# Windowed attention and a gated feed-forward layer on one core: new start-up order for loads, casts, exponentials and masks

## The chip, the core and the metric

The kernel runs on one core of a Trainium2 chip. The metric is the time of one execution on the device in microseconds. The kernel before took 253.31 us, the median of 3 runs (253.07 to 253.32). The profiled execution spans 251.2 us from its first to its last recorded instruction; the times of rows below are counted from the start of that span.

Five engines work at the same time, each through its own queue in order: TensorE (PE; its weight loads are PEld), VectorE (DVE), ScalarE (ACT), GpSimd (POOL) and SyncE (SP). Instructions wait for each other through semaphores.

## The reference, cut to what matters

Two layers follow each other. The first is attention with 4 batches, 8 heads, 768 positions and 64 values a head. A query sees the first 8 positions and the last 96 up to itself; a bias grows with the distance, with its own slope in each head. The second is a feed-forward layer over 3072 tokens with 512 features and 1536 hidden ones.

```python
scores = scale * np.matmul(q, k.transpose(0, 1, 3, 2))
...
keep = is_global | is_local
dist = np.where(is_global & ~is_local, float(n_local), np.abs(rel))
slopes = 2.0 ** (-8.0 * (np.arange(H) + 1) / H)
scores = np.where(keep, scores - slopes[:, None, None] * dist, -1e9)
a = softmax(scores)                        # cut: max, exp, sum written out in the reference
x = np.matmul(a, v)                        # heads side by side: 3072 x 512
gate = np.maximum(x @ w_gate, 0.0)
out = (gate * (x @ w_val)) @ w_out
```

## The kernel before

The sequence of a batch is cut into two halves of 384 queries, so there are eight half-sequences, numbered s = 0 to 7. Heads are taken in pairs p = 0 to 3. Attention of one half is woven into the feed-forward matmuls of an earlier half. At the start there is nothing to weave it into, and the code below lays out by hand in which order every engine works. "Pair" below is a pair of heads of half 0 if nothing else is said.

Loads of half 0, a k and a q transfer for each pair, all from SyncE's queue:

```python
        for src, dst in ((k, ks_of[s]), (q, qs_of[s])):
            nc.sync.dma_start(
                out=dst[:, h0:h1, :],
                in_=src[b, h0:h1, half * QH : (half + 1) * QH, :].rearrange(
                    "h (p n) d -> p h (n d)", n=NN))
```

The pieces for a pair: cast k and q to bf16 (L255), transpose them on TensorE into a PSUM bank (L290), copy the transposed keys (L270 to L272) and queries (L300) to SBUF on VectorE, start the scores' PSUM banks with the distance bias (a matmul of a scaled identity with the distances, L312), add the score matmuls onto them (L330), and take the exponential (L335):

```python
    def piece_cast(s, p, i, eng):
        if (s, p) not in cast_of:
            cast_of[s, p] = cast_pool.tile([128, 2, NN, 2, D], BF16, name="qk")
        src = (qs_of[s], ks_of[s])[i]
        (eng.copy if eng is nc.scalar else eng.tensor_copy)(
            cast_of[s, p][:, i].rearrange("t n e d -> t e n d"),
            src[:, 2 * p : 2 * p + 2, :].rearrange("t e (n d) -> t e n d", n=NN))
...
    def piece_copy(s, p):
        b, half = divmod(s, 2)
        tp = tp_of[s, p]
        put_keys(nc.vector.tensor_copy, nc.vector.tensor_copy, kT[b % 2][p], tp[:, 1, :], half)
        for e in range(2):
            r = slice(64 * e, 64 * e + 64)
            nc.vector.tensor_copy(qTb[s % 2][r, p, e, :], tp[r, 0, :])
...
    def piece_bias(s, p):
        pool, name = (ff_psum, "ff_ps") if s == 0 and p % 2 else (qk_psum, "qk_ps")
        banks = [pool.tile([128, 512], FP32, name=name) for _ in range(3)]
        qk_of[s, p] = banks
        for g, bank in enumerate(banks_of_half[s % 2]):
            c = 0
            for i, (j, a, w, m) in enumerate(bank):
                for e in range(2):
                    nc.tensor.matmul(banks[g][:, c : c + NN * w], lhsT=sid[:, 2 * p + e],
                                     rhs=dd[:, 0 if j == 0 else 1, :, m : m + w],
                                     start=(i == 0 and e == 0), stop=False, skip_group_check=True)
                    c += NN * w

    def piece_biased(s, p):

        b, half = divmod(s, 2)
        kt = kT[b % 2][p]
        qd = qTb[s % 2][:, p].rearrange("d e (n p) -> d e n p", n=NN)
        es01 = es_pool.tile([128, 2, 480], BF16, name="es01")
        es2 = es_pool.tile([128, 480], BF16, name="es2")
        for g, bank in enumerate(banks_of_half[half]):
            ps = qk_of[s, p][g]
            es = es01[:, g] if g < 2 else es2
            c = 0
            for j, a, w, m in bank:
                n_ = 2 * NN * w
                nc.tensor.matmul(ps[:, c : c + n_], lhsT=kt[:, j, :], rhs=qd[:, :, :, a : a + w],
                                 start=False, stop=True, skip_group_check=True)
                for e in range(2):
                    es_of[s, p, j, e] = (es, c + e * NN * w)
                c += n_
            nc.scalar.activation(es[:, 0:c], ps[:, 0:c], AF.Exp, bias=0.0, scale=scale)
```

Where a bias is not used (later halves, and pair 2 of half 1), the exponential is multiplied with a mask made beforehand from the same distances, one mask a head:

```python
    def setup_sid(h):
        nc.scalar.activation(sid[:, h], ident, AF.Copy, bias=0.0, scale=-slopes[h] / scale)

    def setup_mask(h):
        nc.scalar.activation(m_all[:, h], dd, AF.Exp, bias=0.0, scale=-slopes[h])
```

Then row sums (what = 0, with a block of ones as weights) and values (what = 1), two PSUM banks of a pool that has two; ln and exp(-x) on ScalarE give the reciprocal of the sums, and a VectorE product writes xT:

```python
    def piece_av_wide(s, p, pool=av_psum, name="av_ps"):

        b, half = divmod(s, 2)
        todo = [t for bank in banks_of_half[half] for t in bank]
        av = [pool.tile([128, 512], FP32, name=name) for _ in range(2)]
        for what in range(2):
            av3 = av[what][:, 0:QH].rearrange("d (n p) -> d n p", n=NN)
            for i, (j, a, w, m) in enumerate(todo):
                for e in range(2):
                    es, ce = es_of[s, p, j, e]
                    z0 = D + 2 * D * (2 * p + e)
                    nc.tensor.matmul(av3[64 * e : 64 * e + 64, :, a : a + w],
                                     lhsT=ones if what == 0 else vbuf[b % 2][:, j, z0 : z0 + D],
                                     rhs=es[:, ce : ce + NN * w].rearrange("k (n p) -> k n p", n=NN),
                                     start=(i == 0), stop=(i == len(todo) - 1),
                                     skip_group_check=True)
        av_of[s, p] = av

    def piece_norm_wide(s, p):
        av = av_of[s, p]
        ln = rc_pool.tile([128, QH], FP32, name="lnd")
        nc.scalar.activation(ln, av[0][:, 0:QH], AF.Ln, bias=0.0, scale=1.0)
        rc = rc_pool.tile([128, QH], FP32, name="rcp")
        nc.scalar.activation(rc, ln, AF.Exp, bias=0.0, scale=-1.0)
        if s not in xT_of:
            xT_of[s] = xt_pool.tile([128, N_DC, QH], BF16, name="xT")
        nc.vector.tensor_tensor(xT_of[s][:, p, :], av[1][:, 0:QH], rc, op=ALU.mult)
```

The feed-forward pieces: gate is four matmuls and a relu on ScalarE, val is four matmuls and a product on VectorE that writes ht. Each takes one of three PSUM banks (`ffps`, bufs=3).

```python
        def gate(fc, d0=0, d1=N_DC):
            psg = products(f"g{fc % 2}", wg, fc, d0, d1)
            if d1 < N_DC:
                return
            gr = gr_pool.tile([128, QH], BF16, name="grelu")
            nc.scalar.activation(gr, psg[:, 0:QH], AF.Relu, bias=0.0, scale=1.0)
            st["r", fc] = gr
...
        def val(fc, d0=0, d1=N_DC):
            psv = products("v", wv, fc, d0, d1)
            if d1 < N_DC:
                return
            nc.vector.tensor_tensor(ht[:, fc, :], psv[:, 0:QH], st["r", fc], op=ALU.mult)
```

The order of the first half, in which V, P and A are VectorE, GpSimd and ScalarE, `cast(s, p, ek, eq)` casts k on ek and q on eq, AV is row sums, values and norm of a pair, and F0 is the list of feed-forward pieces of half 0:

```python
    load_v_globals(0)
    for j in range(4):
        load_v(0, j)
    load_qk_cast(1)
    load_w_group(0)
    for h in range(2, 6):
        setup_mask(h)
    warm_up(7)
    piece_bias(0, 0)
    cast(0, 0, V, V)
    cast(0, 1, V, V)
    cast(0, 2, A, A)
    piece_t(0, 0)
    piece_copy(0, 0)
    piece_bias(0, 1)
    piece_t(0, 1)
    piece_biased(0, 0)
    piece_copy(0, 1)
    piece_t(0, 2)
    piece_biased(0, 1)
    piece_copy(0, 2)
    cast(0, 3, V, V)
    copy_v_globals(V, 0, 1, 4)
    piece_bias(0, 2)
    piece_biased(0, 2)
    piece_t(0, 3)
    piece_copy(0, 3)
    piece_bias(0, 3)
    AV(0, 0)
    piece_biased(0, 3)
    AV(0, 1)
...                                  # cut: zeroing, loads of v, weights and half 2
    piece_t(1, 0, *QKB)
    AV(0, 2, *QKB)
    piece_copy(1, 0)
    piece_t(1, 1, *FFB)
    AV(0, 3)
    piece_copy(1, 1)
    S1(0)
...                                  # cut: the other pairs of half 1 with F0[0] to F0[8]
    AV(1, 3)
    F0[9]()
    F0[10]()
    F0[11]()
    for h in (0, 1, 6, 7):
        setup_mask(h)
    load_v_half(2)
```

Of the kernel before, what the change touches and what calls it, by code (L numbers as in the profile page):

```python
# [8 lines left out]
FP32 = mybir.dt.float32  # L9
BF16 = mybir.dt.bfloat16  # L10
AF = mybir.ActivationFunctionType
ALU = mybir.AluOpType
# [3 lines left out]
def kernel(  # L16
# [12 lines left out]
    nc = tc.nc  # L29

    B, H, S, D = q.shape
    NG = int(n_global)
# [32 lines left out]
    const = ctx.enter_context(tc.tile_pool(name="const", bufs=1))  # L65
    setupp = ctx.enter_context(tc.tile_pool(name="setupp", bufs=1))
    stage = ctx.enter_context(tc.tile_pool(name="stage", bufs=2))
    cast_pool = ctx.enter_context(tc.tile_pool(name="cast", bufs=3))
    es_pool = ctx.enter_context(tc.tile_pool(name="es", bufs=3))
    rc_pool = ctx.enter_context(tc.tile_pool(name="rc", bufs=2))  # L70
    xt_pool = ctx.enter_context(tc.tile_pool(name="xt", bufs=3))
    ht_pool = ctx.enter_context(tc.tile_pool(name="ht", bufs=2))
# [5 lines left out]
    ff_psum = ctx.enter_context(tc.tile_pool(name="ffps", bufs=3, space=bass.MemoryType.PSUM))  # L78

    ctx.enter_context(tc.manual_schedule())  # L80
    nc.scalar.preload_act_table_set("natural_log_exp_and_others")


    ident = const.tile([128, 128], BF16)
# [20 lines left out]
    def load_qk(s, h0, h1):  # L105
        b, half = divmod(s, 2)
        if s not in qs_of:
            qs_of[s] = stage.tile([128, H, NN * D], FP32, name="qs")
            ks_of[s] = stage.tile([128, H, NN * D], FP32, name="ks")
        for src, dst in ((k, ks_of[s]), (q, qs_of[s])):  # L110
            nc.sync.dma_start(
                out=dst[:, h0:h1, :],
                in_=src[b, h0:h1, half * QH : (half + 1) * QH, :].rearrange(
                    "h (p n) d -> p h (n d)", n=NN))
# [30 lines left out]
    def copy_v_globals(eng, b, j0, j1):  # L145
        t = vbuf[b % 2][0:NG, :, D:].rearrange("p j (h z) -> p j h z", z=2 * D)[:, :, :, 0:D]
        eng.tensor_copy(t[:, j0:j1], t[:, 0:1].to_broadcast([NG, j1 - j0, H, D]))
# [36 lines left out]

    for p in range(HP):
        load_qk(0, 2 * p, 2 * p + 2)
    gsrc = setupp.tile([NG, 2, NN, WQ], FP32)
    gl = setupp.tile([NG, 2, NN, WQ], FP32)
    warm = setupp.tile([128, 128], BF16)
    nc.vector.memset(warm, 0.0)  # L190
    nc.vector.memset(ident, 0.0)
# [9 lines left out]
    for p in range(HP):  # L201
# [16 lines left out]
                            channel_multiplier=1)  # L218

    q1, q2 = [[1, NN], [NN, WQ]], [[0, 2], [-1, NN], [-NN, WQ]]  # L220
    nc.gpsimd.affine_select(out=gl[:, 0], in_=gsrc[:, 0], compare_op=ALU.is_ge, fill=BIG,
                            base=-NL, pattern=q1, channel_multiplier=-1)
    nc.gpsimd.affine_select(out=gl[:, 0], in_=gl[:, 0], compare_op=ALU.is_ge, fill=float(NL),
                            base=0, pattern=q1, channel_multiplier=-1)
    nc.gpsimd.affine_select(out=gl[:, 1], in_=gsrc[:, 1], compare_op=ALU.is_ge, fill=BIG,
                            base=-(NL - 1), pattern=q1, channel_multiplier=0)
    nc.gpsimd.affine_select(out=dd[0:NG], in_=gl, compare_op=ALU.is_ge, fill=BIG,
                            base=NL + KT - 2, pattern=q2, channel_multiplier=0)
# [65 lines left out]
# [7 lines that stand above are left out]
# [237 lines left out]
    def cast(s, p, ek, eq):  # L538
        piece_cast(s, p, 1, ek)
        piece_cast(s, p, 0, eq)  # L540
# [13 lines left out]
    def AV(s, p, *pool):  # L554
        piece_av_wide(s, p, *pool)
        piece_norm_wide(s, p)
# [3 lines left out]
        load_v(0, j)  # L560
    load_qk_cast(1)
    load_w_group(0)
    for h in range(2, 6):
        setup_mask(h)
    warm_up(7)
    piece_bias(0, 0)
    cast(0, 0, V, V)
    cast(0, 1, V, V)
    cast(0, 2, A, A)
    piece_t(0, 0)  # L570
    piece_copy(0, 0)
    piece_bias(0, 1)
    piece_t(0, 1)
    piece_biased(0, 0)
    piece_copy(0, 1)
    piece_t(0, 2)
    piece_biased(0, 1)
    piece_copy(0, 2)
    cast(0, 3, V, V)
    copy_v_globals(V, 0, 1, 4)  # L580
    piece_bias(0, 2)
    piece_biased(0, 2)
    piece_t(0, 3)
    piece_copy(0, 3)
    piece_bias(0, 3)
    AV(0, 0)
    piece_biased(0, 3)
    AV(0, 1)

    zero_q(P, 1)  # L590
# [48 lines left out]
    F0[9]()  # L639
    F0[10]()  # L640
    F0[11]()
    for h in (0, 1, 6, 7):
        setup_mask(h)
    load_v_half(2)
    for p in range(HP):
# [60 lines left out]
```

The softmax here doesn't subtract the row's maximum and nothing guards it: scores larger than these inputs give would overflow.

## Time and profile before

| what | before |
|---|---|
| time, median of 3 runs | 253.31 us |
| span of the profile | 251.2 us |
| TensorE busy | 239.8 us (95%) |
| ScalarE, VectorE, GpSimd busy | 156.8, 137.1, 88.4 us |
| TensorE busy from 0 to 23 us | 17.45 us |
| TensorE busy from 23 to 45 us | 21.84 us |
| TensorE busy from 45 us to the end | 200.56 of 206.20 us |
| granted TensorE clock | full in every slice |

How to read it: busy time is the sum of an engine's instructions, overlaps counted once. A row of a timeline has the start and the duration in us, engine, line of the kernel, operation, out <- in, the count of merged instructions, and in brackets how long the engine was idle ahead of it and what ended that wait. A row of waits says who waited for what, for how long in total, how often, and the longest one. The granted clock being full throughout, no time goes into throttling. The three stretches in the table separate the start, where the attention of half 0 is worked off alone, from the rest.

### The profile page before, as it was taken

How to read it: one execution, taken by the hardware profiler on the slowest of the kernel's cores; microseconds unless marked ns; L12 is line 12 of the kernel's file. 1: busy time of each engine (PE TensorE's matmuls, PEld its weight loads, DVE VectorE, ACT ScalarE, POOL GpSimd, SP SyncE). 2: the span in 40 equal slices, each digit the busy share in tenths (PEclk: the TensorE clock that was granted, in tenths of full speed). 3: DMA queues.
4: the chain of work that ended last, by engine and by line, in shares of the span. 5: the costliest groups of instructions: out<-in, count | busy, mean ns of one | idle time of the engine just before them, and what ended most of it. 6: DMA issues, size and time to landing. Idle time of an engine off the chain costs nothing.

```text
span 251.2 us, 4845 instructions
## 1 busy us (share of the span) xinstructions
PE 239.8 (95%) x1741; PEld 142.5 (57%) x1749; DVE 137.1 (55%) x352; ACT 156.8 (62%) x323; POOL 88.4 (35%) x205
## 2 busy tenths in 40 slices
PE   7679999999999999999999999999999999999993
PEld 4566665556454666556664666556655666556541
DVE  5959557966441467527662567527662557424410
ACT  7886874257654687557774687557774687553321
POOL 8996542059491067202527076203520000000000
PEclk9999999999999999999999999999999999999999
DMA  6999999959699666739468966738432100020012
GB/s 187 166 179 188 207 197 207 145 140 156 77 211 172 193 174 150 53 108 266 104 88 88 248 173 146 55 111 261 104 86 82 43 3 0 19 110 0 0 42 84
DMA packets 77431, 31.56 MB, mean 126 GB/s; under 512 B 57440, under 2 KB 74336, under 8 KB 77408
## 3 DMA queue, kind: packets, MB, share of 16 engines
q0 software_dynamic: 36080, 9.48, 37.1%
q1 hardware_dynamic: 41328, 21.78, 31.7%
q8 instruction: 13, 0.21, 0.4%
q14 instruction: 10, 0.08, 0.1%
HBM read 28.38 MB, written 6.29 MB: 138 GB/s over the span
## 4 chain that ended last, share of the span: by engine, by line
PE 83%; DVE 7%; ACT 6%; DMA 1%; issue 1%; SPq 1%; ACTq 0%
PE ff_ps L478 45%; PE ff_ps L501 24%; PE av_ps L410 5%; PE qk_ps L382 5%; DVE xT L427 2%; DMA qs<-in_q_dram 1%; DVE ht L494 1%; ACT es L335 1%; ACT grelu L487 1%; PE av_ps L441 1%; ACT rcp L424 1%; PE qk_ps L330 1%; ACT lnd L419 1%; DVE qT L300 1%; PE qk_ps L290 1%
## 5 line engine op out<-in xcount | busy, mean ns | idle before, releaser
L478 PE MATMUL ff_ps<-xT,wv 128*128 128x384 bf16 x384 | 78.1, 326 | 0.8 <-DVE ht L494 0.3
L478 PE MATMUL ff_ps<-xT,wg 128*128 128x384 bf16 x384 | 78.1, 326 | 0.0
L487 ACT ACTIVATE grelu<-ff_ps 128x384 bf16<-128x384 f32 x96 | 47.0, 490 | 33.7 <-PE ff_ps L478 13.5
L501 PE MATMUL ff_ps<-wo_sb,ht 128*128 128x512 bf16 x280 | 66.4, 379 | 0.4
L494 DVE TENSOR_TENSOR ht<-ff_ps,grelu 128x384 bf16<-128x384 f32 x96 | 53.2, 555 | 21.5 <-PE ff_ps L478 13.4
L427 DVE TENSOR_TENSOR xT<-av_ps,rcp 64x384 bf16<-64x384 f32 x48 | 26.6, 555 | 46.4 <-ACT rcp L424 41.9
L478 PEld LDWEIGHTS <-wv 128*128 128x128 bf16 x384 | 36.0, 97 | 23.4 <-issue 2.1
L478 PEld LDWEIGHTS <-wg 128*128 128x128 bf16 x384 | 36.0, 97 | 23.0 <-issue 0.2
L394 DVE TENSOR_TENSOR es<-es,m_all 128x432 bf16<-128x432 bf16 (+5 forms) x113 | 34.3, 332 | 26.0 <-ACT es L385 25.2
L385 ACT ACTIVATE es<-qk_ps 128x432 bf16<-128x432 f32 (+2 forms) x75 | 39.5, 529 | 9.4 <-PE qk_ps L382 7.7
L501 PEld LDWEIGHTS <-ht 128*128 128x128 bf16 x288 | 27.0, 97 | 28.3
L419 ACT ACTIVATE lnd<-av_ps 64x384 f32<-64x384 f32 x48 | 23.3, 485 | 13.3 <-PE av_ps L410 12.6
L506 ACT COPY osb<-ff_ps 128x512 f32<-128x512 f32 x24 | 14.1, 586 | 26.7 <-PE ff_ps L501 25.8
L338 POOL CAST kc<-ks 128x384 bf16<-128x384 f32 x20 | 10.0, 544 | 52.6 <-DMA ks<-in_k_dram 52.6
L382 PE MATMUL qk_ps<-qT,kT 128*128 128x432 bf16 (+5 forms) x113 | 25.8, 286 | 0.0
L151 POOL DMA_DIRECT2D vbuf<-in_v_dram x28 | 24.3, 874 | 3.8 <-DMA wg<-in_moe_w_gate_dram 2.4
L410 PEld LDWEIGHTS <-vbuf 128*128 128x128 bf16 x216 | 18.3, 98 | 8.7 <-issue 0.8
L410 PE MATMUL av_ps<-es,vbuf 128*128 128x216 bf16 (+4 forms) x216 | 21.4, 226 | 0.6 <-DVE xT L427 0.6
L382 PEld LDWEIGHTS <-kT 128*128 128x128 bf16 x113 | 10.9, 98 | 7.5
L346 POOL CAST qz<-qs 128x192 bf16<-128x192 f32 x40 | 12.4, 358 | 1.8 <-DMA qs<-in_q_dram 1.8
L424 ACT ACTIVATE rcp<-lnd 128x384 f32<-128x384 f32 x24 | 12.5, 523 | 0.8
L335 ACT ACTIVATE es<-qk_ps 128x432 bf16<-128x432 f32 (+2 forms) x15 | 7.0, 536 | 3.2 <-PE qk_ps L330 3.2
(92 smaller groups left out, 146.1 us busy)
## 6 DMA issues: line engine op xcount, KB each, us to landing
out_dram<-osb SPq DMA_DIRECT2D x24, 256.0 KB
ks<-in_k_dram SPq DMA_DIRECT2D x5, 768.0 KB
qs<-in_q_dram SPq DMA_DIRECT2D x5, 768.0 KB
vbuf<-in_v_dram POOLq DMA_DIRECT2D x24, 120.0 KB, 4.5
wg<-in_moe_w_gate_dram POOLq DMA_DIRECT2D x3, 512.0 KB, 9.1
wv<-in_moe_w_val_dram POOLq DMA_DIRECT2D x3, 512.0 KB, 10.9
wo_sb<-in_moe_w_out_dram POOLq DMA_DIRECT2D x1, 1536.0 KB, 19.1
ks<-in_k_dram SPq DMA_DIRECT2D x4, 192.0 KB
```

The source lines that it names most:

```text
L151: nc.gpsimd.dma_start(out=v_dst(b, NG + r0, NG + r0 + n, j), in_=v[b, :, KT * j + r0 : KT * j + r0 + n, :].rearrange("h p d -> p h d"))
L382: nc.tensor.matmul(ps[:, c : c + n_], lhsT=kt[:, j, :], rhs=qd[:, :, :, a : a + w], start=True, stop=True)
L385: nc.scalar.activation(es[:, 0:cols], ps[:, 0:cols], AF.Exp, bias=0.0, scale=scale)
L394: nc.vector.tensor_mul(e4, e4, mk)
L410: nc.tensor.matmul(av3[:, :, a : a + w], lhsT=vb[:, j, z0 : z0 + 128], rhs=es[:, c : c + NN * w].rearrange("k (n p) -> k n p", n=NN), star ...
L419: nc.scalar.activation(ln[o0 : o0 + 64], av[d0 : d0 + 64, 0:QH], AF.Ln, bias=0.0, scale=1.0)
L424: nc.scalar.activation(rc, ln, AF.Exp, bias=0.0, scale=-1.0)
L427: nc.vector.tensor_tensor(xT_of[s][r, p, :], av_of[s, p, e_][r, 0:QH], rc[r], op=ALU.mult)
L478: nc.tensor.matmul(st[key][:, 0:QH], lhsT=w_of(w, dc, fc), rhs=xT_of[c][:, dc, :], start=(dc == 0), stop=(dc == N_DC - 1))
L487: nc.scalar.activation(gr, psg[:, 0:QH], AF.Relu, bias=0.0, scale=1.0)
L494: nc.vector.tensor_tensor(ht[:, fc, :], psv[:, 0:QH], st["r", fc], op=ALU.mult)
L501: nc.tensor.matmul(ps2, lhsT=ht[:, fc, n * 128 : (n + 1) * 128], rhs=wo_sb[:, fc, :], start=(fc == 0), stop=(fc == N_FC - 1))
```

## The change

Four things are changed together, all of them in the start-up. The q of the first pair is issued from ScalarE's queue, so that it does not stand behind k in SyncE's queue, and the activation table is loaded after that issue. The casts of half 0 are shared out anew: pair 1 goes from VectorE to ScalarE, pair 2 from ScalarE to VectorE but only after the copies of pair 1, and the cast pool has two buffers in place of three; the copy of the global values (L147) goes behind the copies of pair 3. A fourth buffer for exponentials lets the scores of pair 3 be worked off ahead of the attention of pair 0. The masks of heads 2 and 3 are made after the second attention, with four others. The sources of the global distances become smaller and bf16. What is computed stays the same.

```diff
--- before.py
+++ after.py
@@ -65,8 +65,8 @@
     const = ctx.enter_context(tc.tile_pool(name="const", bufs=1))
     setupp = ctx.enter_context(tc.tile_pool(name="setupp", bufs=1))
     stage = ctx.enter_context(tc.tile_pool(name="stage", bufs=2))
-    cast_pool = ctx.enter_context(tc.tile_pool(name="cast", bufs=3))
-    es_pool = ctx.enter_context(tc.tile_pool(name="es", bufs=3))
+    cast_pool = ctx.enter_context(tc.tile_pool(name="cast", bufs=2))
+    es_pool = ctx.enter_context(tc.tile_pool(name="es", bufs=4))
     rc_pool = ctx.enter_context(tc.tile_pool(name="rc", bufs=2))
     xt_pool = ctx.enter_context(tc.tile_pool(name="xt", bufs=3))
     ht_pool = ctx.enter_context(tc.tile_pool(name="ht", bufs=2))
@@ -78,7 +78,6 @@
     ff_psum = ctx.enter_context(tc.tile_pool(name="ffps", bufs=3, space=bass.MemoryType.PSUM))
 
     ctx.enter_context(tc.manual_schedule())
-    nc.scalar.preload_act_table_set("natural_log_exp_and_others")
 
 
     ident = const.tile([128, 128], BF16)
@@ -108,7 +107,8 @@
             qs_of[s] = stage.tile([128, H, NN * D], FP32, name="qs")
             ks_of[s] = stage.tile([128, H, NN * D], FP32, name="ks")
         for src, dst in ((k, ks_of[s]), (q, qs_of[s])):
-            nc.sync.dma_start(
+            eng = nc.scalar if s == 0 and h0 == 0 and src is q else nc.sync
+            eng.dma_start(
                 out=dst[:, h0:h1, :],
                 in_=src[b, h0:h1, half * QH : (half + 1) * QH, :].rearrange(
                     "h (p n) d -> p h (n d)", n=NN))
@@ -184,8 +184,9 @@
 
     for p in range(HP):
         load_qk(0, 2 * p, 2 * p + 2)
-    gsrc = setupp.tile([NG, 2, NN, WQ], FP32)
-    gl = setupp.tile([NG, 2, NN, WQ], FP32)
+    nc.scalar.preload_act_table_set("natural_log_exp_and_others")
+    gsrc = setupp.tile([NG, NN, WQ], BF16)
+    gl = setupp.tile([NG, 2, NN, WQ], BF16)
     warm = setupp.tile([128, 128], BF16)
     nc.vector.memset(warm, 0.0)
     nc.vector.memset(ident, 0.0)
@@ -218,11 +219,11 @@
                             channel_multiplier=1)
 
     q1, q2 = [[1, NN], [NN, WQ]], [[0, 2], [-1, NN], [-NN, WQ]]
-    nc.gpsimd.affine_select(out=gl[:, 0], in_=gsrc[:, 0], compare_op=ALU.is_ge, fill=BIG,
+    nc.gpsimd.affine_select(out=gl[:, 0], in_=gsrc, compare_op=ALU.is_ge, fill=BIG,
                             base=-NL, pattern=q1, channel_multiplier=-1)
     nc.gpsimd.affine_select(out=gl[:, 0], in_=gl[:, 0], compare_op=ALU.is_ge, fill=float(NL),
                             base=0, pattern=q1, channel_multiplier=-1)
-    nc.gpsimd.affine_select(out=gl[:, 1], in_=gsrc[:, 1], compare_op=ALU.is_ge, fill=BIG,
+    nc.gpsimd.affine_select(out=gl[:, 1], in_=gsrc, compare_op=ALU.is_ge, fill=BIG,
                             base=-(NL - 1), pattern=q1, channel_multiplier=0)
     nc.gpsimd.affine_select(out=dd[0:NG], in_=gl, compare_op=ALU.is_ge, fill=BIG,
                             base=NL + KT - 2, pattern=q2, channel_multiplier=0)
@@ -560,31 +561,31 @@
         load_v(0, j)
     load_qk_cast(1)
     load_w_group(0)
-    for h in range(2, 6):
+    for h in range(4, 6):
         setup_mask(h)
     warm_up(7)
     piece_bias(0, 0)
     cast(0, 0, V, V)
-    cast(0, 1, V, V)
-    cast(0, 2, A, A)
+    cast(0, 1, A, A)
     piece_t(0, 0)
     piece_copy(0, 0)
     piece_bias(0, 1)
     piece_t(0, 1)
     piece_biased(0, 0)
     piece_copy(0, 1)
+    cast(0, 2, V, V)
     piece_t(0, 2)
     piece_biased(0, 1)
     piece_copy(0, 2)
     cast(0, 3, V, V)
-    copy_v_globals(V, 0, 1, 4)
     piece_bias(0, 2)
     piece_biased(0, 2)
     piece_t(0, 3)
     piece_copy(0, 3)
+    copy_v_globals(V, 0, 1, 4)
     piece_bias(0, 3)
+    piece_biased(0, 3)
     AV(0, 0)
-    piece_biased(0, 3)
     AV(0, 1)
 
     zero_q(P, 1)
@@ -639,7 +640,7 @@
     F0[9]()
     F0[10]()
     F0[11]()
-    for h in (0, 1, 6, 7):
+    for h in (0, 1, 2, 3, 6, 7):
         setup_mask(h)
     load_v_half(2)
     for p in range(HP):
```

## Prediction

> **What bounds the kernel now.** I read the busy times by stretch first. From 23 to 45 us TensorE is busy 21.84 of 22.00 us; from 45 us to the end 200.56 of 206.20 us, and 4 us of what is missing there is the last output leaving. In the first 23 us it is busy 17.45. So TensorE sets the time, and only two things can change it: how early TensorE reaches its dense stretch (first feed-forward matmul at 22.82 us), and new holes in that stretch. Next come the waits of TensorE in the first 26 us (waiter, line <- releaser: us in total, times, longest):
> ```profile
> PE qk_ps L330 <- DVE qT L300: 1.3, 2, 0.9
> PE ff_ps L242 <- DVE warm L190: 1.0, 1, 1.0
> PE qk_ps L312 <- DVE qT L300: 0.9, 1, 0.9
> PE ff_ps L330 <- DVE qT L300: 0.6, 1, 0.6
> PE av_ps L441 <- ACT lnd L451: 0.6, 1, 0.6
> ```
> The key is that nearly all of them end at VectorE's copies of transposed keys and queries (L270 to L300), or at ScalarE's ln of a softmax sum. The timeline of VectorE (start, duration) shows that chain at work:
> ```profile
> 5.23 0.36 DVE L255 CAST qk<-ks 128x384 bf16<-128x384 f32 x1 [0.21 <-DMA ks<-in_k_dram]
> 5.78 0.65 DVE L255 CAST qk<-qs 128x384 bf16<-128x384 f32 x1 [0.20 <-DMA qs<-in_q_dram]
> 6.36 0.51 DVE L270 COPY kT<-av_ps 128x360 bf16<-128x360 bf16 x1
> ...
> 11.59 0.88 DVE L147 COPY vbuf<-vbuf 8x1536 bf16<-8x1536 bf16 x1
> 12.51 0.53 DVE L270 COPY kT<-av_ps 128x360 bf16<-128x360 bf16 x1
> ...
> 13.17 0.71 DVE L300 COPY qT<-av_ps 64x384 bf16<-64x384 bf16 x2
> ```
> The first pair's copies start at 6.36, because the second pair's casts stand ahead of them; TensorE had ended that pair's transposes at 5.73 (six from 5.23, for 0.50). The timeline of ScalarE shows the other half:
> ```profile
> 13.03 0.49 ACT L451 ACTIVATE lnd<-av_ps 128x384 f32<-128x384 f32 x1 [0.41 <-PE av_ps L441]
> 13.55 0.52 ACT L453 ACTIVATE rcp<-lnd 128x384 f32<-128x384 f32 x1
> 14.36 1.29 ACT L335 ACTIVATE es<-ff_ps 128x432 bf16<-128x432 f32 x3 [0.29 <-PE ff_ps L330]
> 15.53 0.51 ACT L451 ACTIVATE lnd<-av_ps 128x384 f32<-128x384 f32 x1
> 16.07 0.52 ACT L453 ACTIVATE rcp<-lnd 128x384 f32<-128x384 f32 x1
> 16.50 0.47 ACT L451 ACTIVATE lnd<-qk_ps 128x384 f32<-128x384 f32 x1
> ```
> ln and reciprocal of pair 0 use a hole before pair 3's exponentials; from 14.36 to the last reciprocal's end (18.46) ScalarE never stops. Last, the four late masks, ScalarE and then TensorE:
> ```profile
> 35.77 1.91 ACT L237 ACTIVATE m_all<-dd 128x432 bf16<-128x432 bf16 x4
> 37.58 0.89 ACT L487 ACTIVATE grelu<-ff_ps 128x384 bf16<-128x384 f32 x2
> ```
> ```profile
> 38.11 0.81 PE L478 MATMUL ff_ps<-xT,wv 128*128 128x384 bf16 x4 [0.17 <-ACT grelu L487]
> ```
> The relu behind the masks is the one that frees a feed-forward PSUM bank; TensorE already waits 0.17 us for it. There is no slack left there.
>
> **What the Trainium skill says.** DMA: Bandwidth & Descriptors, section "Issuing engines are not separate DMA queues": issuing from several engines only saves sequencer time, all run on the same 16 engines. The trace before fits: an issue on the SyncE queue takes 0.46 us, and issues stand about 0.52 apart. So the ScalarE issue is worth about 0.5 us of arrival and no bandwidth. ScalarE: Activation LUTs, section "What ACT_TABLE_LOAD costs": a load takes about 1283 ns, an ACTIVATE with immediates 186 ns + 0.833 ns an element, and neighbours overlap by about 93 ns. For a 432-wide mask that is an estimate of 546 ns; the trace has the load at 1.28 us, a mask at 0.55, and masks 0.455 apart. Perfetto Trace Analysis, section "Optimization Strategy": a recurring gap can mean that PSUM is short for the next tile. Here it is single gaps, but the cause is that one: the av pool has two banks.
>
> **The change, part by part.**
> 1. *First q from ScalarE's queue, smaller setup.* q of pair 0 is issued at about 0.74 instead of 1.26, later loads 0.5 earlier. TensorE's first real work is the bias (L312), which waits until 4.69 for the masks' distances from GpSimd (an affine_select of 8x216 and one of 128x216 cost 0.36 to 0.39, so narrower types save nothing there). The bias takes until 5.23, and the cast of q ended at 5.02 already. The table load starts 0.5 later; the eight scaled identities then end at 4.2 instead of 3.73, still before 4.69. Worth: 0.
> 2. *Casts.* Pair 1 moves to ScalarE: two masks (4.67 to 5.6), then casts of 0.51 and 0.51, done by 6.6, transposed by 6.9. VectorE is free at 5.75: its first copy starts **0.6 earlier**. A pair's copies take 1.35, 1.61, 1.50 and 1.37 in the timeline, mean 1.46. So copies 0 and 1 end at about 7.1 and 8.55. Now pair 2's casts run on VectorE only then: two of 0.36 to 0.4, ending at 9.35, and the transposes wait for them. The last three transposes and the way back take about 0.4 (three starts 0.055 apart, 0.22 each, signals). Copies 2: 9.75 to 11.2. The same again for pair 3: casts to 12.0, copies 12.4 to 13.85. Before, the last copies ended at 13.88. The head start is eaten by two hand-overs of 0.4 each in which VectorE idles, though the vbuf copy (0.88) was moved behind. Worth at 13.9: 0. The vbuf copy now ends at about 14.7 instead of 12.47.
> 3. *Fourth exp buffer, scores of pair 3 ahead of attention 0.* The built program's order has pair 3's score matmuls, then row sums and values of pair 0; on ScalarE pair 3's exponentials come before ln and reciprocal of pair 0. Those exponentials start at 14.25 (0.4 after the matmuls, as 13.96 to 14.36 before), last 1.29, so ln 0 runs from about 15.4 to 15.9 instead of ending at 13.52. And the order with its waits shows a new one: pair 1's row sums take the bank that ln 0 releases, and pair 1's values the bank that ln 1 releases. TensorE thus waits from 15.1 to **15.95** for the row sums (14.58 before); they take 0.45, ln 1 comes after reciprocal 0 and ends at about 16.95; pair 1's values start at **17.0** (14.88 before). The transposes of the second half and attention 2 follow: row sums of pair 2 end at about 18.0 (15.92 before), ln 2 18.05 to 18.5, reciprocal to 19.1, against 17.52. VectorE's xT of pair 2 and the copies behind it (18.03 to 19.35 before) shift by the same 1.6, and with them the bias at 19.41 that TensorE waits for. Cost: 19.1 less 17.52 is 1.58; with pair 3's start some 0.1 uncertain, **+1.65**. From there everything runs in the same order.
> 4. *Two masks moved.* In front they were beside waits. At 35.8 they lie between the relu that frees a bank and TensorE: 2 x 0.455 = **+0.9**, the wait of 0.17 becoming about 1.1.
>
> Sum: 253.31 + 1.65 + 0.9 = **255.9**; I take 0.1 off for small holes later that may shrink (one of 0.57 at 69.23, some of 0.1 to 0.17): 255.8.
>
> **The rivals.**
> - *The head start is kept.* If VectorE's 0.6 reaches the end, the masks still cost 0.9: 253.6. For it: the copies are what TensorE waits for before 11 us. Against: casts and copies alternate on one engine with TensorE between.
> - *The masks hide.* If ScalarE reaches 35.8 ahead of TensorE, it is 254.9. Against: it waits 0.67 for TensorE before each of the two relus at 33.23 and 35.38, so it is never ahead.
> - *The bank wait isn't there, or smaller*, because attention 0 fits into the hole before the exponentials: about 254.2, masks only. Against: ScalarE's queue is in order, and the exponentials come first.
> - *Weights bind.* The first val weights are issued at 12.70 and take 10.7 us, so they land at 23.4; TensorE needs them at 24.08. A start faster by over 0.7 would stop there; a later one has more room. So no large gain is to be had either way.
>
> **Range and chances.** The front's delay may be 0.8 to 2.3, the masks 0.6 to 1.1, later holes -0.3 to +0.3: 80% from 254.6 to 256.7. Slower by over 2% needs 258.4, 2.6 above the middle: 0.03. Faster by over 2% needs 248.2, more than the 5.55 us that TensorE idles in the first 23 us could give after the masks' cost: 0.01. Within 2%: 0.96.
>
> **What would show it.** Right: VectorE's first L271 copy near 5.75 and pair 3's last query copy near 13.9; TensorE waiting some 0.9 in front of pair 1's row sums and 0.6 or more in front of its values, both on lnd L452; first feed-forward matmul at about 24.5; six masks in a row near 37.5, then a TensorE wait of about 1.1 for grelu L488. Wrong: feed-forward starting before 23, which means that copies of pairs 2 and 3 were not held by the casts or the bank wait fell elsewhere; or a wait under 0.4 after the masks. A third way to be wrong is the first loads: two queues side by side could land k later and hold the first transposes.

## The result and the profile after

| | before | after |
|---|---|---|
| time, median | 253.31 us | 256.35 us (256.25 to 257.66) |
| ratio, 95% interval | | 1.0131 (1.0097 to 1.0166) |
| span of the profile | 251.2 us | 254.4 us |
| first feed-forward matmul (gate) | 22.82 us | 24.47 us |
| TensorE's wait behind the late masks | 0.17 us | 1.06 us |

The kernel is 3.0 us slower, within 2%. The prediction was 255.8 us. Both losses stand where it put them; a third one, of 0.4 us, was not in it.

TensorE's waits in the first 28 us of the changed kernel (waiter, line <- releaser: us in total, times, longest; line numbers are one higher than before):
```profile
PE av_ps L442 <- ACT lnd L452: 1.4, 2, 0.8
PE av_ps L291 <- DVE qk L256: 1.2, 1, 1.2
PE ff_ps L243 <- DVE warm L191: 1.0, 1, 1.0
PE ff_ps L331 <- DVE qT L301: 0.9, 1, 0.9
PE qk_ps L313 <- DVE qT L301: 0.9, 1, 0.9
```
One wait of 0.6 on a softmax sum's ln has become two of 1.4 together, and now heads the list. Waits on copies of queries are still there. The timeline of TensorE (start, duration, and in brackets the idle time ahead of it) puts the two waits in their place, in front of pair 1's row sums and of its values:
```profile
14.47 0.45 PE L442 MATMUL av_ps<-es,ones 128*64 128x216 bf16 x8
14.77 0.43 PE L442 MATMUL av_ps<-es,vbuf 128*64 128x216 bf16 x8
15.98 0.45 PE L442 MATMUL av_ps<-es,ones 128*64 128x216 bf16 x8 [0.78 <-ACT lnd L452]
17.01 0.44 PE L442 MATMUL av_ps<-es,vbuf 128*64 128x216 bf16 x7 [0.58 <-ACT lnd L452]
...
24.47 0.82 PE L479 MATMUL ff_ps<-xT,wg 128*128 128x384 bf16 x4
...
40.65 0.81 PE L479 MATMUL ff_ps<-xT,wv 128*128 128x384 bf16 x4 [1.06 <-ACT grelu L488]
```
The timeline of ScalarE says why: its queue is in order, and pair 3's exponentials stand ahead of the first ln.
```profile
14.25 1.29 ACT L336 ACTIVATE es<-ff_ps 128x432 bf16<-128x432 f32 x3 [1.44 <-PE ff_ps L331]
15.41 0.51 ACT L452 ACTIVATE lnd<-av_ps 128x384 f32<-128x384 f32 x1
15.96 0.52 ACT L454 ACTIVATE rcp<-lnd 128x384 f32<-128x384 f32 x1
16.47 0.49 ACT L452 ACTIVATE lnd<-av_ps 128x384 f32<-128x384 f32 x1
...
37.41 2.81 ACT L238 ACTIVATE m_all<-dd 128x432 bf16<-128x432 bf16 x6
40.13 0.85 ACT L488 ACTIVATE grelu<-ff_ps 128x384 bf16<-128x384 f32 x2
```
ln 0 ends at 15.92, and the row sums start at 15.98. The six masks take 2.81 us in one piece, and the relu that frees the bank follows them. VectorE's timeline shows where the rearranged casts led:
```profile
5.78 0.53 DVE L271 COPY kT<-av_ps 128x360 bf16<-128x360 bf16 x1 [0.82 <-PE av_ps L291]
...
9.71 0.53 DVE L271 COPY kT<-av_ps 128x360 bf16<-128x360 bf16 x1 [0.44 <-PE av_ps L291]
...
12.44 0.53 DVE L271 COPY kT<-av_ps 128x360 bf16<-128x360 bf16 x1 [0.44 <-PE av_ps L291]
13.10 0.71 DVE L301 COPY qT<-av_ps 64x384 bf16<-64x384 bf16 x2
```
The first copy starts 0.58 us earlier than before. Then two waits of 0.44 for TensorE's transposes come in, and the last copy ends at 13.81, against 13.88.

**Where the 3 us come in.** TensorE does the same matmuls in nearly the same order in both kernels, so each can be laid beside its own counterpart. The exception is the column 13.9, pair 3's scores: in the kernels with the new order row sums and values of pair 0 are still to come there, some 0.7 us of work (14.47 to 15.20) that the kernel before has behind it. It is part of their step to the next column. The table has how much later (us) the same piece of work starts than in the kernel before; columns are its time in the kernel before. It carries the reading of most experiments below. The profiled runs of pair 3's scores moved alone and of the masks spread out are among the slower ones of their kernels, so of those two only steps from column to column are read.

| kernel | 13.9 | 22.8 | 38.1 | 65 | 246 |
|---|---|---|---|---|---|
| changed kernel | -0.10 | +1.64 | +2.54 | +2.97 | +3.10 |
| masks alone | +0.09 | +0.10 | +1.00 | +1.00 | +1.02 |
| casts alone | +1.32 | +1.32 | +1.32 | +1.32 | +1.41 |
| order of pair 3 alone | +0.82 | +2.56 | +2.56 | +3.42 | +3.37 |
| first loads alone | +0.07 | +0.07 | +0.07 | +0.07 | +0.26 |
| changed, attention 0 first again | +0.86 | +0.85 | +1.75 | +2.00 | +2.29 |
| changed, other banks | +0.20 | +1.12 | +2.02 | +2.43 | +2.43 |
| changed, masks spread | +1.36 | +3.09 | +2.77 | +3.37 | +3.34 |
| changed, GpSimd tied | +0.07 | +1.81 | +2.71 | +2.73 | +2.48 |

In the changed kernel three steps make up the loss: 1.74 between 13.9 and 22.8, 0.90 at the masks, 0.43 between 38.1 and 65.

### The profile page after: what moved, and what is told of

Same layout as the page of the kernel before. It is cut to its first block, busy times and chain, and to the rows that moved or that the text cites. A ratio compares the mean times of both kernels' runs of the same rounds, so it can differ in the third digit from the quotient of the medians.

```text
span 254.4 us, 4844 instructions
## 1 busy us (share of the span) xinstructions
PE 240.6 (95%) x1741; PEld 142.4 (56%) x1749; DVE 138.6 (54%) x352; ACT 156.7 (62%) x323; POOL 88.3 (35%) x205
## 4 chain that ended last, share of the span: by engine, by line
PE 80%; DVE 7%; ACT 7%; DMA 2%; issue 2%; SPq 0%; ACTq 0%
PE ff_ps L479 43%; PE ff_ps L502 24%; PE av_ps L411 5%; PE qk_ps L383 4%; DVE xT L428 2%; DMA qs<-in_q_dram 2%; DVE ht L495 2%; ACT grelu L488 1%; ACT es L336 1%; DVE qT L301 1%; ACT m_all L238 1%; PE qk_ps L291 1%; ACT rcp L425 1%; ACT lnd L420 1%; PE av_ps L442 1%
## 5 line engine op out<-in xcount | busy, mean ns | idle before, releaser
L395 DVE TENSOR_TENSOR es<-es,m_all 128x432 bf16<-128x432 bf16 (+5 forms) x113 | 35.4, 342 | 25.8 <-ACT es L386 25.1
L420 ACT ACTIVATE lnd<-av_ps 64x384 f32<-64x384 f32 x48 | 23.3, 485 | 13.3 <-PE av_ps L411 12.6
```

The lines of the kernel that those rows point to most:

```text
L395: nc.vector.tensor_mul(e4, e4, mk)
L420: nc.scalar.activation(ln[o0 : o0 + 64], av[d0 : d0 + 64, 0:QH], AF.Ln, bias=0.0, scale=1.0)
```

## The experiments

The theory is the prediction's own. The rivals are that the casts, the first loads or TensorE's clock cause part of the loss. For the last one nothing speaks: the mean granted clock is 0.999 in the trace after and 0.998 in the one before. Four kernels carry one part of the change each, on top of the kernel before; five undo or alter one part of the changed kernel; three look for a better one. Each was timed beside the kernel before, whose median in those series was 253.15 to 253.23 us.

### The masks alone
On top of the kernel before:
```diff
-    for h in range(2, 6):
+    for h in range(4, 6):
-    for h in (0, 1, 6, 7):
+    for h in (0, 1, 2, 3, 6, 7):
```


> The kernel before with nothing changed but the place of two masks (heads 2 and 3 made with four others after the second attention). My theory: the first feed-forward matmul stays at 22.8 us, TensorE's wait for the relu behind the masks grows from 0.17 to about 1.07 us, and the time by 0.9 to 254.2. Rival (two masks hide in ScalarE's idle time, or taking them out of the front starts it earlier): 253.3 or less.

Measured: 254.28 us, ratio 1.0038 (1.0024 to 1.0052). TensorE's timeline at the masks:
```profile
39.11 0.81 PE L478 MATMUL ff_ps<-xT,wv 128*128 128x384 bf16 x4 [1.06 <-ACT grelu L487]
```
It is the wait of the changed kernel to the hundredth. Two masks at this place cost about 1.0 us and gave nothing back at the front: the table has +0.10 ahead of them. They had been free there.

### The casts alone
```diff
-    cast_pool = ctx.enter_context(tc.tile_pool(name="cast", bufs=3))
+    cast_pool = ctx.enter_context(tc.tile_pool(name="cast", bufs=2))
-    cast(0, 1, V, V)
-    cast(0, 2, A, A)
+    cast(0, 1, A, A)
...  (behind piece_copy(0, 1))
+    cast(0, 2, V, V)
```


> The kernel before with the casts alone shared out as in the change (pair 1 on ScalarE behind four masks, pair 2 on VectorE behind the copies of pair 1, two cast buffers). Theory: the first copies start 0.6 earlier, but pair 1's transposes wait for ScalarE until about 7.9 us and pair 2's copies for their own casts, so the last copies of pair 3 end at about 15.2 in place of 13.88, and the time grows by 1.3 to 254.6. Rival (the head start of the copies is kept): 252.7 to 253.3, last copies at 13.3 or earlier.

Measured: 254.52 us, ratio 1.0048 (1.003 to 1.0066). ScalarE's timeline has one reason, VectorE's a second:
```profile
4.76 1.92 ACT L237 ACTIVATE m_all<-dd 128x432 bf16<-128x432 bf16 x4 [1.02 <-POOL dd L227]
...
6.99 0.51 ACT L255 CAST qk<-qs 128x384 bf16<-128x384 f32 x1
```
```profile
6.38 0.53 DVE L270 COPY kT<-av_ps 128x360 bf16<-128x360 bf16 x1 [2.09 <-PE av_ps L290]
...
7.93 0.53 DVE L270 COPY kT<-av_ps 128x360 bf16<-128x360 bf16 x1 [0.17 <-PE av_ps L290]
```
With four masks ahead of them the casts end at 7.50, against 6.81 in the changed kernel, where two masks are gone, and pair 1's copies start at 7.93 in place of 7.25. But the first copy is 0.60 later too (6.38 in place of 5.78), because TensorE's first eight bias matmuls took 1.16 us here and 0.87 there and ended 0.54 later, and VectorE then waits only 0.17 for pair 1. The trace of the changed kernel with attention 0 first (below) has two masks and as slow a bias, and is 0.86 late at 13.9. How the 1.32 divide between the masks and the slow start is therefore open. What is shown is that the parts can't be added up one by one: alone they cost 1.07, 1.31, 1.98 and -0.04 us, 4.3 in all, and together 3.0. The 1.3 between these sums is about the casts' term, and at 13.9 the changed kernel shows none.

### Pair 3's scores first, alone
Fourth exp buffer and `piece_biased(0, 3)` ahead of `AV(0, 0)`; two cast buffers and the small bf16 setup tiles make room for it.
```diff
-    es_pool = ctx.enter_context(tc.tile_pool(name="es", bufs=3))
+    es_pool = ctx.enter_context(tc.tile_pool(name="es", bufs=4))
-    AV(0, 0)
     piece_biased(0, 3)
+    AV(0, 0)
     AV(0, 1)
```


> The kernel before with the fourth buffer for exponentials and the scores of pair 3 ahead of the attention of pair 0, nothing else (two cast buffers and the smaller bf16 setup tiles make the room for it). Theory: ln of pair 0 stands behind pair 3's exponentials and starts at about 15.5 instead of 13.03, pair 1's row sums wait for its bank until about 16.1 instead of 14.58, the last reciprocal of half 0 ends 1.5 later, time 254.8. Rival (same work on every engine, only another order, TensorE gets its scores earlier): 253.3, ln at 15.5 but the feed-forward starting at 22.8.

Measured: 255.19 us, ratio 1.0082 (1.0057 to 1.0107), 0.4 more than expected. The same two waits stand in TensorE's timeline, of the same length:
```profile
16.89 0.45 PE L441 MATMUL av_ps<-es,ones 128*64 128x216 bf16 x8 [0.78 <-ACT lnd L451]
17.93 0.44 PE L441 MATMUL av_ps<-es,vbuf 128*64 128x216 bf16 x7 [0.58 <-ACT lnd L451]
```
In the table the step from 13.9 to 22.8 is 2.56 - 0.82 = 1.74, as in the changed kernel. A further step follows between 38.1 and 65, though this kernel moves no mask: the third loss comes with lateness, not with the masks. The table as a whole says the same: the step is 0 in kernels up to 1.3 late at 38.1, 0.25 at 1.75, and 0.4 to 0.9 from 2.0 on, until GpSimd is tied.

### The first loads alone
q of pair 0 from ScalarE's queue, the table load behind it, small bf16 setup tiles.
```diff
-            nc.sync.dma_start(
+            eng = nc.scalar if s == 0 and h0 == 0 and src is q else nc.sync
+            eng.dma_start(
```


> The kernel before with the first part alone: q of pair 0 issued from ScalarE's queue, the table load behind it, the smaller bf16 setup tiles. Theory: worth nothing in time, 253.3 within 0.3, because the bias matmuls hold TensorE until 5.2 us anyway; GpSimd's first load of v goes out 0.16 earlier and the first val weights land about 0.6 earlier than 23.4, which nothing uses. Rival (half a microsecond of arrival is kept to the end): 252.8.

Measured: 253.17 us, ratio 0.999 (0.9977 to 1.0002). It is worth nothing here, as the prediction had it. One thing it had only named as a risk did happen: k lands later. VectorE's timeline:
```profile
3.91 0.36 DVE L255 CAST qk<-ks 128x384 bf16<-128x384 f32 x1 [0.58 <-DMA ks<-in_k_dram]
```
In all nine traces with the early q VectorE waits for k, and this cast starts at 3.86 to 4.26; in the five without it, at 3.30 to 3.48. It costs nothing because TensorE starts its transposes only behind the bias.

### The changed kernel with attention 0 first again
```diff
+    copy_v_globals(V, 0, 1, 4)     # ahead of pair 3's copies, as before
     piece_bias(0, 2)
     piece_biased(0, 2)
     piece_t(0, 3)
     piece_copy(0, 3)
-    copy_v_globals(V, 0, 1, 4)
     piece_bias(0, 3)
-    piece_biased(0, 3)
     AV(0, 0)
+    piece_biased(0, 3)
     AV(0, 1)
```


> The changed kernel with attention of pair 0 ahead of pair 3's scores again, and the copy of the global values ahead of pair 3's copies again (the order before, all other parts of the change kept). Theory: ln and reciprocal of pair 0 run in the hole before pair 3's exponentials, TensorE's waits for lnd in front of pair 1 (0.78 and 0.58) go away, the copies of pair 3 end at 14.2 instead of 13.8; gain 1.2, time 255.1, feed-forward starting near 23.2. Rival (the shift of the front comes from the casts' new places): 256.3, feed-forward still at 24.4.

Measured: 255.44 us, ratio 1.0085 (1.0055 to 1.0114). The wait on lnd is back to one of 0.6, and the step from 13.9 to 22.8 is gone (0.86 to 0.85). So the order alone makes the 1.74. The median time falls by only 0.9, the median span of the executions by 1.5 (254.5 to 252.95): three of the six executions have 2.4 to 2.7 us outside their span, where 1.8 is usual. In this trace TensorE was already 0.86 late at 13.9, of which 0.82 stood before the copy of the global values. That front varies from run to run; the last section comes back to it.

### The changed kernel with other banks
Pair 1's attention takes two banks of the scores' pool and pair 2's those of the av pool:
```diff
-    AV(0, 1)
+    AV(0, 1, *QKB)
...
-    AV(0, 2, *QKB)
+    AV(0, 2)
```


> The changed kernel with pair 1's attention in the scores' PSUM pool and pair 2's in the av pool (the pools of the two exchanged), order of work unchanged. It takes away the bank wait alone and leaves ln 0 behind pair 3's exponentials. Theory: row sums of pair 1 at 15.1 instead of 15.98, values right behind instead of 17.01, ln 2 at 17.4 instead of 18.12; gain 0.7 of the 1.64 of the front, time 255.6. Rival 1 (the wait for the bank is hidden behind ScalarE's queue): 256.3. Rival 2 (the bank wait is all of it): 254.7.

Measured: 255.36 us, ratio 1.0086 (1.0066 to 1.0106). TensorE's timeline, in front of the values of pairs 2 and 3:
```profile
17.42 0.44 PE L442 MATMUL av_ps<-es,vbuf 128*64 128x216 bf16 x7 [0.35 <-DVE xT L457]
...
19.29 0.45 PE L442 MATMUL av_ps<-es,vbuf 128*64 128x216 bf16 x8 [0.70 <-DVE xT L457]
```
No wait on lnd is left, though ln 0 runs as late as before (15.71 to 16.22), which shows that the bank was the cause. Half of the gain went into two new waits: pair 2's values now stand behind xT of pair 0, whose reciprocal is as late as ever (0.35), and pair 3's values behind xT of pair 2 (0.70). The step shrinks from 1.74 to 0.92. The bank and the late ln are two halves of one loss.

### The changed kernel with its masks spread
One mask behind each of six relus in place of six in a row:
```diff
-    for h in (0, 1, 2, 3, 6, 7):
-        setup_mask(h)
...  (in the weave that follows)
+          [(0.02 + 0.065 * i, lambda h=h: setup_mask(h)) for i, h in enumerate((0, 1, 2, 3, 6, 7))],
```


> The changed kernel with the same six late masks, but one after each of the following relus instead of six in a row. Theory: the wait of 1.06 in front of the feed-forward matmul after the masks goes away and nothing comes in its place: 255.3. Rival (ScalarE's added work is what costs, wherever it stands): 256.3, or waits of 0.1 to 0.2 in front of several feed-forward pieces that add up to 1.

Measured: 255.54 us, ratio 1.0099 (1.0068 to 1.013). TensorE no longer waits for a relu there; the step at 38.1 is -0.32 in place of +0.90. So the masks themselves are not what costs: six of them without a break are.

### The late step: reloading later
The step between 38.1 and 65 lies where GpSimd works on half 3 (fills, casts of k and q) beside VectorE's mask products. The first try put the reload of half 3 later in the weave:
```diff
-          [(0.6, lambda: load_qk_after(3)), (0.6, lambda: load_v_half(3))],
+          [(0.85, lambda: load_qk_after(3)), (0.6, lambda: load_v_half(3))],
```


> The changed kernel with the reload of half 3's q and k triggered some 4 us later. In the changed kernel TensorE loses another 0.44 us between 55 and 62 us, where VectorE's products with the masks take up to 1.29 instead of 0.38 while GpSimd casts keys from 60.12 to 62.2. Theory (GpSimd's work, timed by transfers, has come to lie beside VectorE's products): with the casts later the loss goes away or moves, the three products from 58.7 to 61.4 take 0.4 each again, time 255.9 to 256.0. Rival (VectorE is slow there for another reason): the same loss between 55 and 62 us, 256.3.

Measured: 256.31 us, ratio 1.012 (1.0102 to 1.0139). Nothing follows: GpSimd's casts started at the same time as before, since its own queue holds them and not the reload, and the step is the same.

### The late step: GpSimd tied to VectorE
In the changed kernel VectorE's rows around 60 us stand beside GpSimd's, first VectorE's timeline, then GpSimd's:
```profile
53.42 1.06 DVE L273 COPY kT<-kT 128x56 bf16<-128x56 bf16 x1
...
56.19 0.38 DVE L395 TENSOR_TENSOR es<-es,m_all 128x432 bf16<-128x432 bf16 x1
...
58.71 0.99 DVE L395 TENSOR_TENSOR es<-es,m_all 128x288 bf16<-128x288 bf16 x2 [0.55 <-ACT es L386]
59.62 0.55 DVE L495 TENSOR_TENSOR ht<-ff_ps,grelu 128x384 bf16<-128x384 f32 x1
60.09 1.29 DVE L395 TENSOR_TENSOR es<-es,m_all 128x432 bf16<-128x432 bf16 x1
```
```profile
52.57 0.55 POOL L649 MEMSET vbuf<- 128x544 uint32 x1 [13.78 <-DMA vbuf<-vbuf]
53.07 2.72 POOL L651 MEMSET qz<- 128x1536 uint32 x2
55.74 2.01 POOL L156 MEMSET vbuf<- 128x288 uint32 x7
57.70 2.43 POOL L151 DMA_DIRECT2D vbuf<-in_v_dram  x3
60.12 2.07 POOL L339 CAST kc<-ks 128x384 bf16<-128x384 f32 x4
```
GpSimd's block starts when a transfer of v has landed, at 52.57; in the kernel before at 53.30:
```profile
53.30 0.55 POOL L648 MEMSET vbuf<- 128x544 uint32 x1 [13.78 <-DMA vbuf<-vbuf]
```
TensorE and VectorE are 2.54 later by then, GpSimd 0.73 earlier, so other rows meet. The next kernel moves the block back to where it stood against the others, and the issue of half 3's v with it:
```diff
+    def pool_block():
+        nc.gpsimd.tensor_copy(scr, qTb[0][:, HP - 1, 1, 0:2])   # waits for VectorE's last query copy
+        nc.gpsimd.memset(qz[0]...)                              # one fill repeated, for time
+        ...                                                     # then the fills as they were
-          [(0.6, lambda: load_qk_after(3)), (0.6, lambda: load_v_half(3))],
+          [(0.6, lambda: load_qk_after(3)), (0.97, pool_block), (0.98, lambda: load_v_half(3))],
```


> The changed kernel, with GpSimd's block of fills and casts near 53 us tied to VectorE's query copies of half 2's last pair and preceded by one repeated fill (1.35 us), so that it starts near 55.8 us instead of 52.57, which is where it stood against TensorE's work before the change (53.30 + 2.54). Theory (the last 0.44 us come from GpSimd's block lying beside VectorE's bf16 copies and mask products): the 128x56 key copy takes about 0.2 instead of 1.06 us and the mask product at 60.1 about 0.4 instead of 1.29, TensorE's delay against before stays at 2.55 to 2.65 from 50 to 65 us, and the time is about 255.9. Rival (the 0.44 come from TensorE's own order, PSUM or the clock): the delay grows to 2.98 as before, 256.3.

Measured: 255.7 us, ratio 1.0093 (1.0071 to 1.0114), although GpSimd does more. The same rows of VectorE's timeline:
```profile
53.59 0.18 DVE L273 COPY kT<-kT 128x56 bf16<-128x56 bf16 x1
...
58.80 0.40 DVE L395 TENSOR_TENSOR es<-es,m_all 128x288 bf16<-128x288 bf16 x2 [0.55 <-ACT es L386]
...
59.59 0.37 DVE L395 TENSOR_TENSOR es<-es,m_all 128x432 bf16<-128x432 bf16 x1
```
The copy takes 0.18 in place of 1.06 and the product 0.37 in place of 1.29; GpSimd's fills start at 55.90. TensorE's delay grows by 0.02 between 38.1 and 65 in place of 0.43. The late step is this collision, and it is shown.

### A faster version, with and without the early q
From what came before: casts of pairs 1 and 2 on ScalarE with no mask ahead of them, masks 4 and 5 in ScalarE's hole before half 1's first scores, the others spread, and half 1's first copies ahead of pair 2's norm product. On top of the kernel before:
```diff
-    for h in range(2, 6):
-        setup_mask(h)
-    cast(0, 1, V, V)
-    cast(0, 2, A, A)
+    cast(0, 1, A, A)
...  (behind piece_t(0, 1))
+    cast(0, 2, A, A)
-    AV(0, 2, *QKB)
+    piece_av_wide(0, 2, *QKB)
     piece_copy(1, 0)
+    piece_norm_wide(0, 2)
...  (behind piece_copy(1, 1))
+    for h in (4, 5):
+        setup_mask(h)
-    for h in (0, 1, 6, 7):
-        setup_mask(h)
...  (in the weave)
+          [(0.02 + 0.065 * i, lambda h=h: setup_mask(h)) for i, h in enumerate((0, 1, 2, 3, 6, 7))],
```
The first has the early q and the small setup of the change in addition, the second has not.

> The kernel before, with the first q from ScalarE's queue and the small setup; casts of pairs 1 and 2 both on ScalarE, no mask ahead of them; masks 4 and 5 made in ScalarE's hole just before half 1's first scores, the other six spread one behind each relu; copies of half 1's first pair ahead of pair 2's norm product. Theory: VectorE's first copy near 5.8, its last query copy of pair 3 about 0.8 earlier than before (near 13.1), no wait of 0.9 or 0.6 on lnd of pairs 0 and 1, no wait of over 0.2 after the masks; feed-forward starts near 22.0 and then stands against the weights and v rows of the second half, which land between 22.8 and 24.5, so the gain at the end is 0.8 to 1.0: about 252.4. Rival (weights bind at once): 253.1.

> The same kernel without the first q from ScalarE's queue and without the small setup, so all transfers leave as in the kernel before. Theory: the start is as early, but the val weights land at 23.4 and the v rows near 25.4 as before, so TensorE waits for them and 0.1 to 0.3 are left: about 253.1. Rival (transfers don't bind): within 0.2 of the kernel with the early q, 252.5.

Measured: 252.6 us with the early q, ratio 0.9967 (0.9956 to 0.9979), with the next section's version the fastest of this study; 253.8 without it, ratio 1.0015 (0.9999 to 1.0032). TensorE's timelines, with the early q and then without:
```profile
22.54 0.82 PE L478 MATMUL ff_ps<-xT,wg 128*128 128x384 bf16 x4
23.20 0.76 PE L382 MATMUL qk_ps<-qT,kT 128*128 128x144 bf16 x5
23.79 0.81 PE L478 MATMUL ff_ps<-xT,wv 128*128 128x384 bf16 x4
...
25.52 0.48 PE L441 MATMUL av_ps<-es,vbuf 128*64 128x72 bf16 x10
```
```profile
22.56 0.82 PE L478 MATMUL ff_ps<-xT,wg 128*128 128x384 bf16 x4
23.22 0.76 PE L382 MATMUL qk_ps<-qT,kT 128*128 128x144 bf16 x5
24.04 0.82 PE L478 MATMUL ff_ps<-xT,wv 128*128 128x384 bf16 x4
...
25.78 0.66 PE L441 MATMUL av_ps<-es,vbuf 128*64 128x72 bf16 x10
```
Both reach the feed-forward at the same time, 0.27 earlier than the kernel before. Without the early q, val starts 0.82 behind the scores in place of 0.59 and the v rows stretch the values from 0.48 to 0.66: the first val weights land at 24.0 here (issued at 12.8, 11.2 us), so the transfers bind, as the prediction's fourth rival had said. It had put them at 23.4, though, and expected them to bind only a start faster by over 0.7. So the early q, worth nothing alone, is worth something once the start is faster. Its size is less sure: the medians differ by 1.2 us, the two traces by 0.44 at 65 and by 0.8 at 246. The second half of that comes from a hole of 0.31 at 72.98 in the kernel without it, which the next section explains.

### The warm-up


> The best kernel so far with eight warm-up matmules in place of seven, so that TensorE works until about 4.6 us and waits 0.1 to 0.2 for the distances instead of 0.57. In the traces the first pair's eight bias matmuls took 0.69 us in some runs and 1.16 in others, with the same work ahead of them, and all seven warm-up matmuls are slow (0.634 us each) where they took 1.16. Theory (TensorE is still slow because its warm-up ends too early): the eight take about 0.7 and the six transposes 0.5 in place of 0.8, VectorE's first copy starts near 5.9 instead of 6.58, feed-forward starts near 22.0, where the val weights (landing near 23.2) leave 0.2 to 0.5 of it: about 252.2. Rival (the slowness has another cause, a transfer or another engine): 1.16 again, 252.6.

Measured: 252.57 us, ratio 0.9972 (0.9959 to 0.9985), the same as the version with seven. The start of its TensorE timeline:
```profile
1.39 3.19 PE L242 MATMUL ff_ps<-warm 128*128 128x512 bf16 x7
4.53 1.13 PE L312 MATMUL qk_ps<-dd,sid 128*128 128x216 bf16 x8
5.51 0.49 PE L290 MATMUL av_ps<-ident,qk 128*128 128x128 bf16 x6
```
The wait ahead of the bias is gone, and the bias still takes 1.13. The expectation of 0.7 was wrong, though the transposes behind it take 0.49 in place of 0.80, and feed-forward starts at 22.07, as hoped. The time did not follow. TensorE was 1.08 us ahead of the kernel before at 65 us, and then meets one new hole in its timeline:
```profile
72.16 0.20 PE L382 MATMUL qk_ps<-qT,kT 128*128 128x48 bf16 x1 [0.40 <-POOL kT L275]
```
GpSimd again, from the other side: it keeps its own time, so a TensorE that is early waits for its key copies. What counts is the one against the other. GpSimd's block starts at 53.57 here, 0.27 later than before the change; in the version without the early q it starts at 54.27, 0.97 later, and TensorE is 0.17 early: a hole of 0.31. In the version with seven it starts 0.27 earlier, TensorE is 0.61 early, and there is no hole.

## Why the prediction held, and where it fell short

- **First loads, 0.** Held: 253.17 us for that part alone, although k lands some 0.5 later. That they would become worth something in a faster kernel was only said as "weights bind".
- **Casts, 0 at 13.9 us.** Held in the changed kernel: first copy at 5.78 (5.75 predicted), last copy ends at 13.81 (13.85), both hand-overs 0.44 (0.4). That the last copy met 13.85 so closely is partly luck: the four other kernels with the same work up to there stand between -0.13 and +1.36 at 13.9 in their traces. The prediction reckoned the casts behind two masks and then gave the moving of the other two no credit in front; the casts alone, behind four, cost 1.3 us, of which the masks' share is open.
- **Order of pair 3, +1.65.** Held: 1.64 at the first feed-forward matmul, with waits of 0.78 and 0.58 where about 0.9 and 0.6 were expected. The steps between stand too: values of pair 1 at 17.01 (17.0), ln 2 at 18.12 (18.05), its reciprocal done at 19.16 (19.1). Restoring the order takes the step away; other banks take away its first half and move part of it to xT.
- **Two masks, +0.9.** Held: 0.90 in the table, a wait of 1.06 (1.1).
- **Later holes, -0.1.** This term failed, in sign too. It looked only at TensorE's own holes, which a delay might shrink. It measured +0.43 up to 65 us and +0.13 from there, 0.56 in all and outside its own range of -0.3 to +0.3. The prediction took it that after 19 us "everything runs in the same order", each engine shifted alike. GpSimd's block did not shift, and VectorE's copies and products ran into it.
- **The sum.** 1.64 + 0.90 + 0.56 = 3.10, against 3.04 between the medians. The range from 254.6 to 256.7 holds 256.35; the middle was low by 0.55, which is about the failed term (+0.56 in place of -0.1).
- **Of the rivals**, the head start was not kept, the masks did not hide, and the bank wait was there. Weights bound nothing in a later start, only in an earlier one, and there sooner than said: a start 0.27 faster was enough.

## What to carry to other kernels

Before work is moved ahead on an engine with an in-order queue, look at what stands behind it there and releases a buffer: here three early exponentials delayed one ln, and with it a PSUM bank that TensorE was to write next. Work that is free beside a wait is not free in a dense stretch, but the same work cut into single pieces between the instructions that release buffers may be. After every shift ask which engine does not shift with the rest, and what it will then lie beside.

## What the runs showed of the hardware that was not expected

- **VectorE beside GpSimd.** A product of two bf16 operands in SBUF (128x432) took 0.38 us beside GpSimd's fills (at 56.19 above) and 1.29 beside its casts; two of 288 took 0.99 in place of 0.40 beside GpSimd's issue of transfers; a 128x56 copy within SBUF took 1.06 in place of 0.18 beside a fill. The ht product in between, which reads PSUM, stayed at 0.55. The Trainium skill, SBUF — State Buffer, section "🔬 SBUF: two separate sides", says that only VectorE and GpSimd share a pair of ports, that it is a lock for a whole instruction, which the one that starts first gets, and no sharing of bandwidth, and that products with both inputs in SBUF take part in it only against GpSimd's reads. The fills only write and the casts read SBUF, so the product's 0.38 and 1.29 agree; whether an issue of transfers reads SBUF, no trace here shows. Who starts first shows at the front: in the nine traces with the early q VectorE's first cast and GpSimd's last select (8x432) overlap. Where the cast started first it took 0.36 and the select 0.75 to 0.79; where the select did, it took 0.57 and the cast 0.43 to 0.77. What is shown of the late step by experiment is that moving GpSimd's block moves the slow rows.
- **TensorE's first work runs at half pace.** In every trace the warm-up matmuls of 512 columns start 0.40 to 0.43 us apart; late in the kernel they start 0.216 apart. The bias matmuls of 216 columns start 0.180 apart before a certain moment and 0.092 after it. This moment differs between the 14 traces: before the first bias in four (its eight matmuls took 0.69 us, in the kernel before among others), within it in three (0.83 to 0.98, the changed kernel's 0.87 among them), at its end or behind it, between 5.4 and 6.7 us, in seven (1.13 to 1.17). In the trace with the masks spread the half pace comes back from 9.9 to 13.3 us. This is part of what makes the fronts of single traces differ, by up to 1.3 us at 9.4 between changed kernels with the same work so far. The granted clock, full in every slice of the kernel before, does not show it, so it can't be taken to mean that no time is lost to a slow start. The eighth warm-up matmul was tried once, and the bias still began at half pace; what sets the moment was not tested.
- **Narrower types.** GpSimd's first two selects of 8x216 took 0.36 us in bf16 as in f32. The third took 0.53 in f32 and 0.36 in the changed kernel, but VectorE's cast lay beside it in the first (from 3.47) and not in the second (from 3.93); beside a cast it took 0.47 in bf16.
